# A dense layer with Mish on one core: the head of the program in smaller pieces (x tiles 0 and 1, k 0 of w1)

## The chip, the core and the metric

The kernel runs on one core of one Trainium2 chip. Time is device time in microseconds (us) of one execution; what is compared is the median over runs. The core's engines are TensorE (PE, with its weight loads listed apart as PEld), VectorE (DVE), ScalarE (ACT), GpSimd (POOL) and SyncE (SP). SP and ACT each have a ring (a queue) from which 16 DMA engines take transfers.

## The reference: two matrix products with Mish between

```python
B, S, D, F = 1, 2048, 512, 1792          # all inputs bf16
h = jnp.einsum("bsd,df->bsf", x, w1) + b1
sp = jnp.log1p(jnp.exp(-jnp.abs(h))) + jnp.where(h > 0, h, jnp.zeros_like(h))
act = h * jnp.tanh(sp)
return jnp.einsum("bsf,fd->bsd", act, w2)
```

## The kernel before

The 2048 rows of x are four blocks of 512. Within a block, the first product makes h transposed: w1 is the stationary side, in 4 slices of 128 along D (called k 0 to 3) and 14 slices of 128 along F (called f 0 to 13); xT, x transposed, is the moving side. Each (block, f) adds four products of k 0 to 3 into one bank of PSUM, and ScalarE reads the bank, adds b1 and applies Mish into `a_sb`. The second product takes `a_sb` as the stationary side and w2 as the moving one, 14 products for each tile of 128 rows; VectorE copies the bank out and SP stores it. All blocks go through PE in the order in which the code is written: first products of block 0, second products of block 0, first products of block 1 and so on. There is no planner: each engine takes its instructions in the order of the code, and waits are semaphore counts (`wait`, `mark`).

Only the head, block 0, is special. Its 512 rows are four tiles of 128, called tile 0 to 3 (`j` or `js` in the code).

- Tiles 2 and 3, and all later blocks, come in transposed by a DMA transpose. Tiles 0 and 1 come as they are into `x_nat` and are transposed on PE against an identity matrix (`ident`), in halves of 64 rows (`transpose_x`, product at L147), 16 small products; VectorE and ScalarE copy the results from PSUM to xT (L155).
- While these loads are under way PE runs 7 filler products on constants (L105, sizes in `WARM`).
- For f 0 to 7 (`OPEN` = 8, one bank each) w1 comes in four loads, one for each k: k 0 and k 2 on ScalarE's ring (L109 and L110), k 1 and k 3 on SP's (L112 and L115), k 3 behind the DMA transpose of tiles 2 and 3 (L114). That transpose waits for the third filler.
- SP's ring then has b1, w1 for f 8 to 13, w2 and the transposes of blocks 1 to 3.
- `first(fs, js, ks)` (L239) writes products of block 0 for those f, tiles and k; `mm1_step` (L168) puts the waits ahead of each: the bank, the load of w1, the copy of xT.

Tiles 0 and 1 are read with two neighbouring rows of x in one partition: partition p holds row 2p as tile 0 and row 2p + 1 as tile 1, so one load of 256 KB has rows of 2 KB. `rows` (L191) stores these two tiles accordingly.

Of the kernel before, what the change touches and what calls it, by code (L numbers as in the profile page):

```python
# [4 lines left out]

P = 128
SQ = 32
WARM = (512,) * 5 + (256,) * 2
BLOCKS = (512, 512, 512, 512)


# [21 lines left out]
def bass_standalone__dense_activation_mish__prompt_kernel(  # L33
# [16 lines left out]
    x2, out2 = x[0], out[0]  # L50
# [3 lines left out]
    OPEN = 8  # L54
    N0 = BLOCKS[0] // P

    with ExitStack() as es:
        def sb(name, shape, t):
            return es.enter_context(nc.sbuf_tensor(name, shape, t))

        x_nat = sb("x_nat", [P, 2, D], BF)
        xT = sb("xT", [P, KT, S], BF)
# [6 lines left out]
        ident = sb("ident", [P, P], BF)  # L69
        a_sb = sb("a_sb", [P, FT, S], BF)  # L70
        o_sb = sb("o_sb", [P, S // P, D], BF)
        ps = es.enter_context(nc.psum_tensor("ps", [P, 8, 512], F32))

        def sem(name):
            return es.enter_context(nc.semaphore(name))

        sp = Stream(nc.sync, None)
        pe = Stream(nc.tensor, sem("c_pe"))
        dve = Stream(nc.vector, sem("c_dve"))
        act = Stream(nc.scalar, sem("c_act"))  # L80
        pool = Stream(nc.gpsimd, sem("c_pool"))

        def load(q, dst, src, name, transpose=False):
            s = sem(name)
            (q.eng.dma_start_transpose if transpose else q.eng.dma_start)(dst, src).then_inc(s, 16)
            return (s, 16)

        def load_w1(q, ks, a, b):
            return load(q, w1_sb[:, ks, a * P:b * P], w1v[:, ks, a * P:b * P], "s_w1_%d_%d" % (ks.start, a))
# [6 lines left out]
        def load_part(q, k0, k1, a, b):  # L96
            t = load_w1(q, slice(k0, k1), a, b)
            for f in range(a, b):
                for k in range(k0, k1):
                    t_w1[k, f] = t  # L100
# [3 lines left out]
        c_m = nc.const_aps.tensor(1.0, [P, 512], BF)  # L104
        t_fill = [pe.mark(nc.tensor.matmul(ps[:, 7, 0:n], c_w, c_m[:, 0:n], start=True, stop=True)) for n in WARM]  # L105

        act.eng.preload_act_table(ACT.Mish)  # L107
        act.wait(t_bz)
        for k in (0, 2):  # L109
            load_part(act, k, k + 1, 0, OPEN)  # L110
        t_xn = load(sp, x_nat[:, :, :], x2[0:2 * P, :].rearrange("(p j) d -> p j d", p=P), "s_xn")
        load_part(sp, 1, 2, 0, OPEN)  # L112
        sp.wait(t_fill[2])
        t_x23 = load(sp, xT[:, :, 2 * P:4 * P], x2[2 * P:4 * P, :], "s_x23", True)  # L114
# [4 lines left out]
        t = load(sp, w2_sb[:, :, :], w2v, "s_w2")  # L119
# [3 lines left out]
        for s in range(1, len(BLOCKS)):  # L123
            lo, hi = starts[s], starts[s + 1]
# [5 lines left out]
        t_id = dve.mark(nc.vector.tensor_scalar(ident[:, :], diff[:, :], 0, None, ALU.is_equal))  # L130

        free = [[] for _ in range(8)]
        t_cp = {(j, k): t_x23 for j in (2, 3) for k in range(KT)}
        t_mish = {}

        def transpose_x():

            pe.wait(t_xn, t_id)
            H = P // 2
            for b0, eng, js, ks in ((0, dve, (0,), (0,)), (2, act, (1,), (0,)), (4, dve, (0, 1), (1,)), (6, act, (0, 1), (2, 3))):  # L140
                m = len(js)
                for i, k in enumerate(ks):
                    for n, j in enumerate(js):
                        lo = (i * m + n) * H
                        for h in (0, 1):
                            g = slice(h * H, (h + 1) * H)
                            mm = nc.tensor.matmul(ps[:, b0 + h, lo:lo + H], x_nat[g, j, k * P:(k + 1) * P], ident[g, g],  # L147
                                                  start=True, stop=True)
                eng.wait(pe.mark(mm))
                for i, k in enumerate(ks):  # L150
                    dst = xT[:, k, js[0] * P:(js[-1] + 1) * P].rearrange("p (j h t) -> p j h t", j=m, h=2)
                    src = ps[:, b0:b0 + 2, i * m * H:(i + 1) * m * H].rearrange("p h (j t) -> p j h t", j=m)
                    if m == 1:
                        dst, src = dst[:, 0], src[:, 0]
                    t = eng.mark(nc.vector.tensor_copy(dst, src) if eng is dve else act.eng.activation(dst, src, ACT.Copy))  # L155
                    for j in js:
                        t_cp[j, k] = t
                free[b0] = free[b0 + 1] = [t]

        def mish(s, f, bank, t_mm):  # L160
            n = BLOCKS[s]
            act.wait(t_b1c, t_mm)
            t = act.mark(act.eng.activation(a_sb[:, f, starts[s]:starts[s + 1]], ps[:, bank, 0:n], ACT.Mish,  # L163
                                            bias=b1_sb[:, f:f + 1]))
            t_mish[s, f] = t
            free[bank] = [t]

        def mm1_step(s, f, k, bank, js=None):  # L168

            n = BLOCKS[s]  # L170
            lo, hi = (0, n) if js is None else (js[0] * P, (js[-1] + 1) * P)
            first = k == 0 and lo == 0
            if first:
                pe.wait(*free[bank])
            pe.wait(t_w1[k, f])
            if s:
                pe.wait(t_xT[s])
            else:
                pe.wait(*[t_cp[j, k] for j in (js or range(N0))])
            return nc.tensor.matmul(ps[:, bank, lo:hi], w1_sb[:, k, f * P:(f + 1) * P],  # L180
                                    xT[:, k, starts[s] + lo:starts[s] + hi], start=first, stop=(k == KT - 1 and hi == n))
# [8 lines left out]

        def rows(i):  # L191

            if i < 2:
                return out2[0:2 * P, :].rearrange("(p j) d -> p j d", p=P)[:, i, :]
            return out2[i * P:(i + 1) * P, :]

        def mm2_step(i, f, lo, hi, bank):
# [7 lines left out]
        def put(i, lo, hi, bank, t_mm, q=sp):  # L205
            nonlocal n_out
            dve.wait(t_mm)
            t = dve.mark(nc.vector.tensor_copy(o_sb[:, i, lo:hi], ps[:, bank, 0:hi - lo]))  # L208
            free[bank] = [t]
            q.wait(t)  # L210
            q.eng.dma_start(rows(i)[:, lo:hi], o_sb[:, i, lo:hi]).then_inc(s_out, 16)
            n_out += 1
# [8 lines left out]
        def mm2_last(i):  # L221

            nonlocal n_out
            cuts = (0, D - 3 * P // 2, D - P // 2, D)
            toks = []
            for n, eng in enumerate((dve, dve, act)):
                lo, hi, bank = cuts[n], cuts[n + 1], 4 + (i + n) % 4
                for f in range(FT):
                    mm = mm2_step(i, f, lo, hi, bank)
                eng.wait(pe.mark(mm))  # L230
                dst, src = o_sb[:, i, lo:hi], ps[:, bank, 0:hi - lo]
                t = eng.mark(nc.vector.tensor_copy(dst, src) if eng is dve else act.eng.activation(dst, src, ACT.Copy))  # L232
                toks.append((lo, hi, t))
            for q, (lo, hi, t) in zip((sp, sp, act), toks):
                q.wait(t)
                q.eng.dma_start(rows(i)[:, lo:hi], o_sb[:, i, lo:hi]).then_inc(s_out, 16)
                n_out += 1

        def first(fs, js, ks, last=False):  # L239
            for k in ks:  # L240
                for f in fs:
                    mm = mm1_step(0, f, k, f % 8, js)
                    if last and k == KT - 1:
                        mish(0, f, f % 8, pe.mark(mm))


        def spread_b1():
            dve.wait(t_b1)
            for j in range(P // SQ):
                t = dve.mark(nc.vector.transpose(b1_T[j * SQ:(j + 1) * SQ, :], b1_nat[:, j * SQ:(j + 1) * SQ]))  # L250
            dve.wait(t)
            return dve.mark(nc.vector.tensor_copy(b1_sb[:, :], b1_T[:, 0:FT]))  # L252

        transpose_x()
        t_b1c = spread_b1()
        first(range(4), (0,), (0,))
        first(range(4), (1,), (0,))
        first(range(4, OPEN), (0, 1), (0,))
        first(range(OPEN), (0, 1), (1, 2))
        first(range(OPEN), (2, 3), (0, 1, 2))  # L260
        first(range(OPEN), None, (3,), True)
        for f in range(OPEN, FT):
# [41 lines left out]
```

## Time and profile before

| what | value |
|---|---|
| time, median of 3 runs | 105.19 us (105.11 to 105.49) |
| span of the profiled execution, first to last instruction | 102.9 us (no time of it beyond the span is listed; the median is 2.3 above) |
| granted TensorE clock, mean | 1.000 |
| busy: PE / PEld | 100.2 us (97%) / 48.8 us (47%) |
| busy: ACT / DVE | 39.5 us (38%) / 13.1 us (13%) |
| read from HBM / written | 3.94 MB / 2.10 MB |

A row of a list of instructions has line, engine, operation, out<-in and shape. In a timeline a row starts with the start in the span and the length in us. A DMA row gives the size and the us from the issue to the landing of the transfer. In the profile, w1_sb and w2_sb are both called `w_sb`, and b1_nat `b_nat`. A matmul's listed length includes its passage through the array, so the step from one matmul to the next is shorter than its length.

### The profile page before, as it was taken

The page shows a single profiled execution, that of the slowest core. Times are in us where ns is not written, and L with a number is a line of the kernel's source. Part 1 is how long each engine was busy: PE and PEld are TensorE (multiplying, and loading weights), DVE is VectorE, ACT ScalarE, POOL GpSimd, SP SyncE. Part 2 cuts the span into 40 slices and gives each one's busy share as a digit, 9 for nine tenths or more (in the row PEclk, how much of TensorE's full clock was granted, in tenths as well). Part 3 has the DMA queues.
Part 4 walks back from the last instruction along what each step waited for, and adds up shares of the span by engine and source line. Part 5 has one row for each costly group of instructions (what it writes and reads, how often), then busy time and mean ns, then how long its engine had stood idle before and what let it go on. Part 6 is the DMA issues. An engine that isn't in the chain of part 4 may idle for free.

```text
span 102.9 us, 1196 instructions
## 1 busy us (share of the span) xinstructions
PE 100.2 (97%) x527; PEld 48.8 (47%) x527; DVE 13.1 (13%) x26; ACT 39.5 (38%) x61; POOL 0.4 (0%) x5
## 2 busy tenths in 40 slices
PE   6999999999999999999999999999999999999993
PEld 2697444444444444444444444444444444444472
DVE  1203000220220000022220000022201000020241
ACT  4301999000047777000017777400006777700000
POOL 1000000000000000000000000000000000000000
DMA  2999999991110000011001000001111000001112
GB/s 61 375 283 358 363 243 112 269 237 51 51 51 0 0 6 0 0 51 51 20 31 51 0 0 10 0 3 48 51 51 51 0 0 0 0 6 51 51 51 51
DMA packets 12977, 7.94 MB, mean 77 GB/s; under 512 B 7980, under 2 KB 12332, under 8 KB 12972
## 3 DMA queue, kind: packets, MB, share of 16 engines
q1 hardware_dynamic: 12540, 7.33, 27.4%
q10 hardware_dynamic: 432, 0.54, 1.5%
q8 instruction: 4, 0.07, 0.3%
q14 instruction: 1, 0.01, 0.0%
HBM read 3.94 MB, written 2.10 MB: 59 GB/s over the span
## 4 chain that ended last, share of the span: by engine, by line
PE 97%; DVE 0%; ACT 0%; issue 0%
PE ps L180 47%; PE ps L202 47%; PE ps L105 3%; DVE xT L155 0%; ACT o_sb L232 0%; PE ps L147 0%
## 5 line engine op out<-in xcount | busy, mean ns | idle before, releaser
L163 ACT ACTIVATE a_sb<-ps,b_sb 128x512 bf16<-128x512 f32 x56 | 37.1, 698 | 47.9 <-PE ps L180 47.9
L180 PE MATMUL ps<-xT,w_sb 128*128 128x512 bf16 (+2 forms) x252 | 49.1, 355 | 0.2 <-DVE xT L155 0.2
L202 PE MATMUL ps<-w_sb,a_sb 128*128 128x512 bf16 (+3 forms) x252 | 49.1, 355 | 0.0
L180 PEld LDWEIGHTS ps<-xT,w_sb 128*128 128x128 bf16 x252 | 24.2, 98 | 24.1 <-DVE xT L155 0.3
L202 PEld LDWEIGHTS ps<-w_sb,a_sb 128*128 128x128 bf16 x252 | 23.2, 98 | 25.5
L208 DVE CAST o_sb<-ps 128x512 bf16<-128x512 f32 x15 | 10.4, 692 | 79.8 <-PE ps L202 79.8
L232 ACT ACTIVATE o_sb<-ps 128x64 bf16<-128x64 f32 x1 | 0.2, 224 | 11.5 <-PE ps L202 11.5
L105 PE MATMUL ps<-const-bfloat16-1.0 128*128 128x512 bf16 (+1 forms) x7 | 2.7, 566 | 0.8 <-PEq L289 0.8
L105 PEld LDWEIGHTS ps<-const-bfloat16-1.0 128*128 128x128 bf16 x7 | 0.9, 138 | 2.1 <-issue 2.1
L155 ACT ACTIVATE xT<-ps 128x256 bf16<-128x256 f32 (+1 forms) x3 | 0.9, 347 | 1.7 <-PE ps L147 1.7
L107 ACT ACT_TABLE_LOAD x1 | 1.3, 1283 | 0.7 <-PEq L289 0.7
L250 DVE STREAM_TRANSPOSE b_T<-b_nat 32x32 bf16<-32x32 bf16 x4 | 0.8, 202 | 3.3 <-DMA b_nat<-in_b_dram 3.2
L232 DVE CAST o_sb<-ps 128x320 bf16<-128x320 f32 (+1 forms) x2 | 0.8, 392 | 1.5 <-PE ps L202 1.5
L155 DVE CAST xT<-ps 128x128 bf16<-128x128 f32 (+1 forms) x2 | 0.6, 354 | 2.4 <-PE ps L147 2.4
L147 PEld LDWEIGHTS ps<-ident,x_nat 64*128 64x128 bf16 x16 | 0.4, 118 | 0.4 <-DMA x_nat<-in_x_dram 0.4
L147 PE MATMUL ps<-ident,x_nat 64*128 64x64 bf16 x16 | 0.5, 222 | 0.0
L130 DVE TENSOR_SCALAR ident<-diff 128x128 bf16<-128x128 int32 x1 | 0.2, 227 | 0.2 <-POOL diff L128 0.2
L128 POOL IOTA diff<- 128x128 int32 x1 | 0.2, 234 | 0.4 <-POOLq L289 0.4
L102 DVE MEMSET b_nat<- 32x64 uint32 x1 | 0.1, 112 | 0.8 <-PEq L289 0.8
L252 DVE CAST b_sb<-b_T 128x14 f32<-128x14 bf16 x1 | 0.2, 176 | 0.0
L289 POOL MEMSET const-bfloat16-1.0<- 128x1 bf16 x1 | 0.1, 102 | 0.0
L289 POOL MEMSET const-uint8-127<- 128x1 uint8 x1 | 0.1, 102 | 0.0
(2 smaller groups left out, 0.2 us busy)
## 6 DMA issues: line engine op xcount, KB each, us to landing
out_dram<-o_sb SPq DMA_DIRECT2D x15, 128.0 KB, 1.7
w_sb<-in_w_dram SPq DMA_DIRECT2D x1, 1792.0 KB, 10.7
w_sb<-in_w_dram SPq DMA_DIRECT2D x1, 768.0 KB, 6.1
w_sb<-in_w_dram ACTq DMA_DIRECT2D x2, 256.0 KB, 3.7
w_sb<-in_w_dram SPq DMA_DIRECT2D x2, 256.0 KB, 3.7
x_nat<-in_x_dram SPq DMA_DIRECT2D x1, 256.0 KB, 2.6
out_dram<-o_sb SPq DMA_DIRECT2D x1, 80.0 KB, 1.6
xT<-in_x_dram SPq DMA_TRANSPOSE x4, 5.0
```

Source lines behind the costliest of these rows:

```text
L105: t_fill = [pe.mark(nc.tensor.matmul(ps[:, 7, 0:n], c_w, c_m[:, 0:n], start=True, stop=True)) for n in WARM]
L107: act.eng.preload_act_table(ACT.Mish)
L128: t_diff = pool.mark(pool.eng.iota(diff[:, :], pattern=[[1, P]], base=0, channel_multiplier=-1))
L130: t_id = dve.mark(nc.vector.tensor_scalar(ident[:, :], diff[:, :], 0, None, ALU.is_equal))
L147: mm = nc.tensor.matmul(ps[:, b0 + h, lo:lo + H], x_nat[g, j, k * P:(k + 1) * P], ident[g, g], start=True, stop=True)
L155: t = eng.mark(nc.vector.tensor_copy(dst, src) if eng is dve else act.eng.activation(dst, src, ACT.Copy))
L163: t = act.mark(act.eng.activation(a_sb[:, f, starts[s]:starts[s + 1]], ps[:, bank, 0:n], ACT.Mish, bias=b1_sb[:, f:f + 1]))
L180: return nc.tensor.matmul(ps[:, bank, lo:hi], w1_sb[:, k, f * P:(f + 1) * P], xT[:, k, starts[s] + lo:starts[s] + hi], start=first, stop=( ...
L202: return nc.tensor.matmul(ps[:, bank, 0:hi - lo], a_sb[:, f, i * P:(i + 1) * P], w2_sb[:, f, lo:hi], start=(f == 0), stop=(f == FT - 1))
L208: t = dve.mark(nc.vector.tensor_copy(o_sb[:, i, lo:hi], ps[:, bank, 0:hi - lo]))
L232: t = eng.mark(nc.vector.tensor_copy(dst, src) if eng is dve else act.eng.activation(dst, src, ACT.Copy))
L250: t = dve.mark(nc.vector.transpose(b1_T[j * SQ:(j + 1) * SQ, :], b1_nat[:, j * SQ:(j + 1) * SQ]))
```

## The change

x tiles 0 and 1 are plain tiles of 128 rows now, loaded by two transfers of 128 KB with rows of 1 KB; `rows` is simplified with it. k 0 of w1 comes as two loads, f 0 to 3 and f 4 to 7, both on ScalarE's ring, ahead of k 2. One filler of 256 columns is left out. PE transposes tile 0 when tile 0 is there (k 0, then k 1 to 3), then tile 1; VectorE copies k 0 of each tile, ScalarE k 1 to 3 of each tile in one instruction. The first products are written in another order.

```diff
-WARM = (512,) * 5 + (256,) * 2
+WARM = (512,) * 5 + (256,)
+HALF = 4
...
-        for k in (0, 2):
-            load_part(act, k, k + 1, 0, OPEN)
-        t_xn = load(sp, x_nat[:, :, :], x2[0:2 * P, :].rearrange("(p j) d -> p j d", p=P), "s_xn")
+        load_part(act, 0, 1, 0, HALF)
+        load_part(act, 0, 1, HALF, OPEN)
+        load_part(act, 2, 3, 0, OPEN)
+        t_xn = [load(sp, x_nat[:, i, :], x2[i * P:(i + 1) * P, :], "s_xn%d" % i) for i in range(2)]
         load_part(sp, 1, 2, 0, OPEN)
         sp.wait(t_fill[2])
         t_x23 = load(sp, xT[:, :, 2 * P:4 * P], x2[2 * P:4 * P, :], "s_x23", True)
...
-            pe.wait(t_xn, t_id)
             H = P // 2
-            for b0, eng, js, ks in ((0, dve, (0,), (0,)), (2, act, (1,), (0,)), (4, dve, (0, 1), (1,)), (6, act, (0, 1), (2, 3))):
+            pe.wait(t_id)
+            for i in (0, 1):
+                pe.wait(t_xn[i])
+                for eng, b0, ks in ((dve, 2 * i, (0,)), (act, 4 + 2 * i, (1, 2, 3))):
...
-            if i < 2:
-                return out2[0:2 * P, :].rearrange("(p j) d -> p j d", p=P)[:, i, :]
             return out2[i * P:(i + 1) * P, :]
...
-        first(range(4), (0,), (0,))
-        first(range(4), (1,), (0,))
-        first(range(4, OPEN), (0, 1), (0,))
-        first(range(OPEN), (0, 1), (1, 2))
+        first(range(HALF), (0,), (0,))
+        first(range(HALF), (1,), (0,))
+        first(range(HALF), (0, 1), (1,))
+        first(range(HALF, OPEN), (0, 1), (0, 1))
+        first(range(OPEN), (0, 1), (2,))
         first(range(OPEN), (2, 3), (0, 1, 2))
         first(range(OPEN), None, (3,), True)
```

On PE, from the transposes to the products of k 2, before (s_xn, s_xn0 and s_xn1 are the loads of x; s_w1_1_0 is k 1 of w1, s_w1_0_0 and s_w1_0_4 k 0, s_w1_2_0 k 2; c_dve and c_act are the copies):

```order
L147 MATMUL ps<-ident,x_nat 128x64 [waits c_dve,s_xn]
L147 MATMUL ps<-ident,x_nat 128x64 x15
L180 MATMUL ps<-xT,w1_sb 128x128 [waits s_w1_0_0,c_dve]
L180 MATMUL ps<-xT,w1_sb 128x128
L180 MATMUL ps<-xT,w1_sb 128x128 [waits c_act]
L180 MATMUL ps<-xT,w1_sb 128x128 x5
L180 MATMUL ps<-xT,w1_sb 128x256 [waits c_dve]
L180 MATMUL ps<-xT,w1_sb 128x256
L180 MATMUL ps<-xT,w1_sb 128x256 [waits c_act]
L180 MATMUL ps<-xT,w1_sb 128x256
L180 MATMUL ps<-xT,w1_sb 128x256 [waits s_w1_1_0]
```

and in the changed kernel:

```order
L149 MATMUL ps<-ident,x_nat 128x64 [waits s_xn0,c_dve]
L149 MATMUL ps<-ident,x_nat 128x64 x7
L149 MATMUL ps<-ident,x_nat 128x64 [waits s_xn1]
L149 MATMUL ps<-ident,x_nat 128x64 x7
L181 MATMUL ps<-xT,w1_sb 128x128 [waits s_w1_0_0,c_dve]
L181 MATMUL ps<-xT,w1_sb 128x128
L181 MATMUL ps<-xT,w1_sb 128x128 [waits c_dve]
L181 MATMUL ps<-xT,w1_sb 128x128 x5
L181 MATMUL ps<-xT,w1_sb 128x256 [waits c_act,s_w1_1_0]
L181 MATMUL ps<-xT,w1_sb 128x256 x3
L181 MATMUL ps<-xT,w1_sb 128x256 [waits s_w1_0_4]
```

All 16 transposes still stand ahead of the first product, the second eight behind a wait of their own. The wait for k 1 stood four 256-column products behind the eight of 128 columns; now it stands right behind them.

On ScalarE's ring, before and then in the changed kernel:

```order
L85 DMA w1_sb<-in_w1_dram 128x1024 [waits c_dve]
L85 DMA w1_sb<-in_w1_dram 128x1024
L155 ACTIVATE xT<-ps 128x128 [waits c_pe]
L155 ACTIVATE xT<-ps 128x256 [waits c_pe]
L155 ACTIVATE xT<-ps 128x256
```

```order
L86 DMA w1_sb<-in_w1_dram 128x512 [waits c_dve]
L86 DMA w1_sb<-in_w1_dram 128x512
L86 DMA w1_sb<-in_w1_dram 128x1024
L156 ACTIVATE xT<-ps 128x3x128 [waits c_pe] x2
L164 ACTIVATE a_sb<-ps,b1_sb 128x512 [waits c_pe,c_dve]
```

ScalarE issues three loads instead of two, k 2 as the third, and makes two copies of 384 columns instead of three of 128, 256 and 256.

On SP's ring, in the changed kernel, up to w1 for f 8 to 13:

```order
L86 DMA x_nat<-in_x_dram 128x512 [waits barrier_Pool_Activation_PE_DVE_SP_release]
L86 DMA x_nat<-in_x_dram 128x512
L86 DMA w1_sb<-in_w1_dram 128x1024
L86 DMA_TRANSPOSE xT<-in_x_dram 128x4x256 [waits c_pe]
L86 DMA w1_sb<-in_w1_dram 128x1024
L86 DMA b1_nat<-in_b1_dram 14x128 [waits c_dve]
L86 DMA w1_sb<-in_w1_dram 128x4x768
```

Before, one load of x stood where the first two stand now; k 1 has moved from the second place to the third, and from there on the queue is the same.

More of the change, by code (lines that the diff above doesn't have):

```diff
@@ L136, in transpose_x @@
         def transpose_x():
-            pe.wait(t_xn, t_id)
             H = P // 2
-            for b0, eng, js, ks in ((0, dve, (0,), (0,)), (2, act, (1,), (0,)), (4, dve, (0, 1), (1,)), (6, act, (0, 1), (2, 3))):
[L141 to L144, printed above, removed]
+            pe.wait(t_id)
+            for i in (0, 1):
+                pe.wait(t_xn[i])
+                for eng, b0, ks in ((dve, 2 * i, (0,)), (act, 4 + 2 * i, (1, 2, 3))):
+                    m = len(ks)
+                    for n, k in enumerate(ks):
                         for h in (0, 1):
                             g = slice(h * H, (h + 1) * H)
[L147 to L152, printed above, removed]
+                            mm = nc.tensor.matmul(ps[:, b0 + h, n * H:(n + 1) * H], x_nat[g, i, k * P:(k + 1) * P],
+                                                  ident[g, g], start=True, stop=True)
+                    eng.wait(pe.mark(mm))
+                    dst = xT[:, ks[0]:ks[-1] + 1, i * P:(i + 1) * P].rearrange("p k (h t) -> p k h t", h=2)
+                    src = ps[:, b0:b0 + 2, 0:m * H].rearrange("p h (k t) -> p k h t", k=m)
                     if m == 1:
@@ L155, in transpose_x @@
                     t = eng.mark(nc.vector.tensor_copy(dst, src) if eng is dve else act.eng.activation(dst, src, ACT.Copy))
-                    for j in js:
-                        t_cp[j, k] = t
-                free[b0] = free[b0 + 1] = [t]
+                    for k in ks:
+                        t_cp[i, k] = t
+                    free[b0] = free[b0 + 1] = [t]
         def mish(s, f, bank, t_mm):
```

## The prediction, on record before the changed kernel ran

> **What bounds the kernel now.** I read the chain of waits first: what follows what until the end, as start, length and work.
>
> ```profile
> 0.77 2.72 PE ps L105 x7
> 3.49 0.19 PE ps L147 x3
> ...
> 3.70 0.30 DVE xT L155
> ...
> 4.13 12.32 PE ps L180 x84
> 16.45 12.09 PE ps L202 x56
> ...
> 88.97 12.17 PE ps L202 x84
> ```
>
> From 4.13 on TensorE (PE) never stops until it has done all products; nothing but its own work is on the chain. So a change at the head of the program counts by one thing: by how much the unbroken run of products is moved. A stall of PE behind 4.13 is paid in full, and an earlier start is won only if PE doesn't stop again.
>
> Next the list of waits, for what PE waits on before 4.13, and the timeline of the head (start, length, engine, line, work).
>
> ```profile
> PEld ps L147 <- DMA x_nat<-in_x_dram: 0.4, 1, 0.4
> PE ps L180 <- DVE xT L155: 0.2, 1, 0.2
> ```
>
> ```profile
> 3.07 0.42 PE L105 MATMUL ps<-const-bfloat16-1.0 128*128 128x256 bf16 x1
> 3.42 0.42 PEld L147 LDWEIGHTS ps<-ident,x_nat 64*128 64x128 bf16 x16 [0.41 <-DMA x_nat<-in_x_dram]
> 3.70 0.62 DVE L155 CAST xT<-ps 128x128 bf16<-128x128 f32 x2 [2.38 <-PE ps L147]
> 3.75 0.91 ACT L155 ACTIVATE xT<-ps 128x128 bf16<-128x128 f32 x3 [1.74 <-PE ps L147]
> ...
> 4.57 4.97 PE L180 MATMUL ps<-xT,w_sb 128*128 128x256 bf16 x44
> ...
> 9.38 7.07 PE L180 MATMUL ps<-xT,w_sb 128*128 128x512 bf16 x32
> ```
>
> PE waits for x at 3.42 and for the first copy at 4.13; the eight 128-column products fill 4.13 to 4.57 (55 ns each); then come 44 products of 256 columns, 4.57 to 9.38, so 109 ns each. The first four of them are k 0 of f 4 to 7, so k 1 of w1 is first used at 4.57 + 4 x 0.109 = 5.01.
>
> Last the DMA view, in narrow windows, so that one transfer stands in each (size, then us from issue to landing; in this order x, k 0, k 1, k 2, the DMA transpose, the rest of w1):
>
> ```profile
> x_nat<-in_x_dram SPq DMA_DIRECT2D x1, 256.0 KB, 2.6
> ...
> w_sb<-in_w_dram ACTq DMA_DIRECT2D x1, 256.0 KB, 3.0
> w_sb<-in_w_dram SPq DMA_DIRECT2D x1, 256.0 KB, 3.6
> ...
> w_sb<-in_w_dram ACTq DMA_DIRECT2D x1, 256.0 KB, 4.3
> ...
> xT<-in_x_dram SPq DMA_TRANSPOSE x1, 4.4
> ...
> w_sb<-in_w_dram SPq DMA_DIRECT2D x1, 768.0 KB, 6.1
> ```
>
> with the issues themselves:
>
> ```profile
> 0.74 0.40 SPq L85 DMA_DIRECT2D x_nat<-in_x_dram  x1
> 0.95 0.38 ACTq L85 DMA_DIRECT2D w_sb<-in_w_dram  x1
> 1.19 0.42 SPq L85 DMA_DIRECT2D w_sb<-in_w_dram  x1
> 1.36 0.46 ACTq L85 DMA_DIRECT2D w_sb<-in_w_dram  x1
> ...
> 2.24 1.31 SPq L85 DMA_TRANSPOSE xT<-in_x_dram  x1
> ...
> 4.73 0.41 SPq L85 DMA_DIRECT2D w_sb<-in_w_dram  x1
> ```
>
> x is there at 0.74 + 2.6 = 3.34, k 0 at 3.95, k 1 at 1.19 + 3.6 = 4.79, k 2 at 5.66, the transposed tiles 2, 3 at 6.64. Today k 1 has 5.01 - 4.79 = 0.22 us to spare. The transfers pass one after another, as the two queues (q1 is SP's, q10 ScalarE's) show in the windows 2.40 to 2.80, 2.85 to 3.40, 3.60 to 4.00 and 4.40 to 4.80 (packets, MB, share of the 16 engines; of each window the one queue that fills it):
>
> ```profile
> q1 hardware_dynamic: 74, 0.15, 93.6%
> ...
> q10 hardware_dynamic: 101, 0.21, 101.1%
> ...
> q1 hardware_dynamic: 72, 0.15, 100.0%
> ...
> q10 hardware_dynamic: 75, 0.15, 99.0%
> ...
> ```
>
> x, then k 0, then k 1, then k 2: whole transfers in the order of issue, alternating between the rings, on 16 engines that are full. So when k 1 lands depends on the bytes ahead of it: 256 KB of x and 256 KB of k 0.
>
> **The change part by part.** *Loads.* x becomes two loads of 128 KB, k 0 two of 128 KB. By the steps of today's issues (0.45 on SP, 0.41 on ScalarE) they go out at 0.74 and 1.19 on SP and 0.95 and 1.36 on ScalarE; k 1 follows on SP at about 1.64, k 2 on ScalarE at about 1.77. The order of passage is then x 0, k 0 low half, x 1, k 0 high half, k 1, k 2: the bytes ahead of k 1 are the 512 KB of before, now in rows of 1 KB instead of 2 KB. k 1's issue is 0.45 later, which costs nothing by itself: it lands 3.6 after issue against x's 2.6, so about 1.0 of it is queueing, and that covers the 0.45. SP's DMA transpose waits for the third filler matmul and goes out at 2.24 as before, since SP is done with k 1 by 1.64 + 0.42 = 2.06.
>
> What 1 KB rows cost: w2 comes in such rows, and 2 KB rows pass from 2.40 to 3.40 (columns: stretch, its length, busy time and count of PE, PEld, DVE, ACT, POOL, clock, DMA share, GB/s).
>
> ```profile
> 1.60:2.40 0.80, 0.80 (x3) 0.28 (x2) 0.00 (x0) 0.41 (x1) 0.00 (x0) 1.00 0.74 125
> 2.40:3.40 1.00, 1.00 (x4) 0.30 (x2) 0.00 (x0) 0.00 (x0) 0.00 (x0) 1.00 1.01 381
> 10.80:13.40 2.60, 2.60 (x14) 1.16 (x12) 0.00 (x0) 2.60 (x6) 0.00 (x0) 1.00 1.09 358
> ...
> DMA packets 593, 0.61 MB, mean 380 GB/s; under 512 B 2, under 2 KB 593, under 8 KB 593
> ```
>
> 512 KB take 1.38 us at 381 GB/s, 1.46 at 358 (w2 behind 10.80) and 1.38 at 380 (the last row, w2 from 10.00 to 11.60): 0 to 0.09 more. The ramp, 1.60 to 2.40, moves only 125 GB/s, 0.10 MB. If it is a matter of time, 1 KB rows lose nothing there; if it is one of a number of rows, they move 0.05 MB in it, and 0.05 MB at 381 GB/s is 0.13 us. Bounds for k 1: 4.79 to 5.01; I take the middle, 4.90. A gain is not in these bounds, since no byte ahead of k 1 is gone.
>
> A rule of the Trainium skill (DMA: Bandwidth & Descriptors, Issuing engines are not separate DMA queues) speaks against the two rings: transfers from both interleave on the same 16 engines, and only issue time is saved. The queue rows agree that the engines are shared, but show whole blocks, not an even mixture; by an even mixture k 1 would share the engines with k 2, which is a rival below.
>
> *Fillers, transposes, copies.* The weights of the third and of the fifth filler of 512 columns:
>
> ```profile
> 1.58 0.15 PEld L105 LDWEIGHTS ps<-const-bfloat16-1.0 128*128 128x128 bf16 x1 [0.28 <-issue]
> ...
> 2.43 0.15 PEld L105 LDWEIGHTS ps<-const-bfloat16-1.0 128*128 128x128 bf16 x1 [0.28 <-issue]
> ```
>
> So one of 512 columns takes 0.85 / 2 = 0.43, one of 256 columns 0.21. One of 256 goes: PE is free at 3.07 instead of 3.28; today it then waits on to 3.42, so the filler was covered by the wait for x, and without that wait it would be worth 0.21. x 0 can be there a little before 3.34, and its eight transposes (half of the 0.42) go early. But both tiles' transposes stand ahead of all products on PE, so the first product waits for x 1. With k 0's low half ahead, x 1 is the third of three 128 KB pieces: 384 KB must pass where 256 KB sufficed for 3.34. 128 KB at 380 GB/s are 0.34, so x 1 lands at about 3.7, transposes start 0.08 behind (3.42 - 3.34) at 3.78; 3.34 and 3.42 are the lower ends, if x 1 passes right behind x 0. The form of each copy:
>
> ```profile
> L155 DVE CAST xT<-ps 128x128 bf16<-128x128 f32 x1 | 0.3, 292 | 2.4 <-PE ps L147 2.4
> L155 ACT ACTIVATE xT<-ps 128x128 bf16<-128x128 f32 x1 | 0.3, 278 | 1.7 <-PE ps L147 1.7
> L155 ACT ACTIVATE xT<-ps 128x256 bf16<-128x256 f32 x2 | 0.7, 381 | 0.0
> ```
>
> VectorE copies k 0 of x 1: from first transpose to product today 4.13 - 3.42 = 0.71, so 4.49. Two products of x 0 are done by then; the third waits, because f 2 and f 3 accumulate in the banks that held x 1's k 0. Six products of 55 ns follow: PE stands before k 1 at 4.49 + 0.33 = 4.82. ScalarE's copy of x 1's k 1 to 3 ends as late: it starts today 3.75 - 3.42 = 0.33 behind the first of four transposes and now has eight ahead of it, so 0.33 + 4 x 0.026 = 0.44 (0.42 / 16 for one); 384 columns take about 0.48 (278 and 381 give 103 ns per 128 columns); to PE it is 4.13 - 3.70 - 0.29 = 0.14: 3.78 + 0.44 + 0.48 + 0.14 = 4.84. VectorE's second copy of 256 columns is gone, and nothing queues behind it but the spreading of b1.
>
> *Order of the products.* Here is the step that decides. Before, k 0 of f 4 to 7 (4 x 0.109 = 0.44 us) stood between the 128-column products and k 1. Now k 1 of f 0 to 3 stands right behind them, and k 0 of f 4 to 7 after it. PE needs k 1 at 4.82 and has it at 4.90 + 0.08 = 4.98 (bounds 4.87 to 5.09). Behind that wait stands the whole rest: the 4.57 point of before. So the run of products is moved by 4.98 - 4.57 = 0.41; without k 1's wait by 4.82 - 4.57 = 0.25.
>
> *Everything later.* k 2 is needed 12 products on, at 4.98 + 1.31 = 6.29, and lands by 5.66 + 0.22 = 5.88; tiles 2, 3 at 6.29 + 0.87 = 7.16 against 6.86; the rest of w1 (4.73 + 6.1 = 10.83 today) against the end of eight 512-column products, 9.38 + 8 x 0.216 = 11.11 plus 0.41 (12.09 / 56 for one). Their cover is the later PE itself. The Mish row, the second products and the stores are as before; tiles 0 and 1 are stored as plain rows, amid the run, where nobody waits.
>
> The sum: span 102.9 + 0.41 = 103.3. The median, 105.19, is 2.3 above the span, and I leave that as it is: 105.19 + 0.41 = 105.6.
>
> **The rivals.** *k 1 in time*: if the ramp is no longer and the order of blocks leaves k 1 at 4.79, the copies of x 1 set the time, +0.25: 105.4. For it: the bounds touch it. Against: any of the two row-size costs.
>
> *The split pays*: x 1 passes right behind x 0 and k 1 comes with the copies. PE could go on from 3.07 + 0.71 = 3.78 at best, 0.35 before 4.13: 104.8, no further, since the fillers end there. Against: k 1 would have to land near 4.2 with the same bytes ahead.
>
> *k 2 ahead of k 1, or mixed with it* (slower): the blocks alternate by issue, and k 1's new issue at 1.64 is only 0.13 ahead of k 2's 1.77. If ScalarE's third issue is ready first, 256 KB at 381 GB/s, 0.69, pass before k 1: 105.6 + 0.69 = 106.3; an even mixture comes to at most the same. It decides from the point where SP's two small loads take longer than ScalarE's two by 0.13. Against: SP began 0.21 earlier today.
>
> *The clock of PE comes late* (slower). Filler matmuls of 512 columns stand 0.43 apart, the products behind 16.45 12.09 / 56 = 0.216 apart. So PE ran at half rate until some point between 3.07 and 4.13, 2.3 to 3.4 us behind its start (the clock column shows 1.00 throughout and cannot tell). The new head has a filler less and three gaps up to 4.98. If full rate needs the same time again from x 1's transposes at 3.78, it comes at 6.1 to 7.2, and half the work from 4.98 on is lost: 0.6 to 1.1, so about 106.4. The Trainium skill (TensorE: Matmul & The Clock Gate, Part 1) has such a rule: full clock follows about 3.4 us of sustained work, in a free-running window. The trace agrees with that length within its bounds, but no row shows what gaps of 0.5 us do.
>
> **How the numbers follow.** Forecast 0.60, k 1 in time 0.17, the split pays 0.06, k 2 first 0.08, late clock 0.09. About 0.5%, 0.53 us, is what can be told from no change here. The forecast with its bounds (+0.30 to +0.52, and some tenths of spread between runs: 105.11 to 105.49) lies mostly below 105.72; a quarter of it, 0.15, and the two slow rivals, 0.17, make slower 0.32. Faster would need 104.66, beyond the best case: 0.02. The rest, 0.66, is no change. The likeliest time is 105.6; its own range is 105.4 to 105.8. The range of 8 in 10 leaves out the best case and the far part of the slow ones: 105.1 to 106.2.
>
> **What would show it.** x 0's transposes near 3.1 and x 1's near 3.8; a wait of PE on w1 (k 1) right behind the 128-column products, ending at 4.9 to 5.1; the 44 products of 256 columns starting 0.3 to 0.5 later than 4.57; the span near 103.3. Wrong if x 1's transposes start before 3.6, if PE runs from the first product without a gap, if q10 moves k 2 ahead of k 1, or if the 256-column products are 0.2 apart.

## The result and the profile after

The changed kernel takes 109.37 us (median of 6 runs, 108.28 to 109.67) against 105.15 (104.36 to 105.49); the ratio is 1.040, with a 95% interval of 1.034 to 1.046. That is 4.2 us slower; forecast were 0.41 us, with a range that ended at 106.2. The profiled execution's span is 108.0 us; it took 109.28. Single executions of one kernel can lie 1 to 2 us apart (106.42 and 104.77 of run s2 below), so ratios leave out those over 1.5% above the fastest, and what rests on one execution is weaker than a median.

The chain of waits after, as start, length and work:

```profile
1.66 6.26 DMA w_sb<-in_w_dram
7.92 0.04 issue
7.96 13.55 PE ps L181 x76
21.52 12.09 PE ps L201 x56
...
94.03 12.17 PE ps L201 x84
```

From 21.52 on the program is the one of before, 21.52 - 16.45 = 5.07 us later. All of the loss lies ahead of it, in two pieces. First, k 1 of w1, issued at 1.66, lands at 7.92, and PE stands for it. Second, the 76 products behind that take 13.55, where before the same 76 (44 of 256 columns and 32 of 512) took 16.45 - 4.57 = 11.88: 1.67 more. (The profiled execution of before is one of its shortest, so 5.07 is more than the 4.2 between the medians.) The head in the timeline:

```profile
3.21 0.40 PE L149 MATMUL ps<-ident,x_nat 64*128 64x64 bf16 x8
3.80 0.39 PE L149 MATMUL ps<-ident,x_nat 64*128 64x64 bf16 x8 [0.20 <-DMA x_nat<-in_x_dram]
4.13 1.12 PE L181 MATMUL ps<-xT,w_sb 128*128 128x128 bf16 x8
7.96 4.68 PE L181 MATMUL ps<-xT,w_sb 128*128 128x256 bf16 x26 [2.71 <-DMA w_sb<-in_w_dram]
```

Tile 0 is transposed from 3.21, tile 1 from 3.80, and the first product starts at 4.13, where it started before. The run of 256-column products, at 4.57 before, starts at 7.96: 3.39 later. 3.39 + 1.67 = 5.06, the whole difference.

What the transfers did in the meantime, by stretches, first of the kernel before and then of the changed one (the last two columns are the packets' time as a share of that of the 16 DMA engines, and GB/s):

```profile
3.20:4.20 1.00, 0.83 (x20) 0.52 (x19) 0.50 (x2) 0.45 (x2) 0.00 (x0) 1.00 1.04 391
4.20:5.20 1.00, 1.00 (x14) 0.93 (x14) 0.13 (x1) 0.46 (x2) 0.00 (x0) 1.00 1.07 343
```

```profile
3.20:4.20 1.00, 0.81 (x18) 0.55 (x18) 0.41 (x2) 0.49 (x1) 0.00 (x0) 1.00 0.97 160
4.20:5.20 1.00, 1.00 (x8) 0.62 (x8) 0.17 (x1) 0.49 (x1) 0.00 (x0) 1.00 0.70 217
5.20:6.20 1.00, 0.05 (x1) 0.00 (x0) 0.00 (x0) 0.00 (x0) 0.00 (x0) 1.00 2.08 252
6.20:7.20 1.00, 0.00 (x0) 0.00 (x0) 0.00 (x0) 0.00 (x0) 0.00 (x0) 1.00 0.77 125
```

From 3.20 to 4.20 the share is about that of before (0.97 against 1.04), but the engines move 160 GB/s instead of 391. So it is not that more bytes stood ahead of k 1; the bytes passed at under half the rate. The share adds up the times of the packets, and it goes above 1 (2.08 from 5.20 to 6.20), so it doesn't say that the engines were full of work. The single packets in the traces show where the time went. A packet of 2 KB takes 84 ns at the median, before and after. But of the 1 and 2 KB packets that start from 2.50 to 6.00, none takes over 0.3 us before, and 16 of 564 do after, the longest 2.30 us; from 3.20 to 4.20 ten such packets make up 8.7 of the 15.4 us that all packets took.

Each of these loads reports its landing in 16 parts, and PE can use it from the last on. Before, the parts of k 1 come within 0.4 us, 4.45 to 4.83. After, they come from 4.67 to 7.92, and those of k 0's high half from 3.77 to 6.37. So the first part of k 1 is there only 0.2 later than before; what PE stands for is the last.

And PE's clock, in stretches of the changed kernel (the third column from the right):

```profile
4.13:5.10 0.97, 0.97 (x12) 0.69 (x8) 0.24 (x1) 0.50 (x2) 0.00 (x0) 1.00 0.72 210
5.10:7.90 2.80, 0.15 (x2) 0.00 (x0) 0.00 (x0) 0.00 (x0) 0.00 (x0) 1.00 1.20 166
8.00:8.60 0.60, 0.60 (x6) 0.54 (x7) 0.00 (x0) 0.00 (x0) 0.00 (x0) 1.00 1.35 360
8.70:12.00 3.30, 3.30 (x17) 2.24 (x16) 0.98 (x5) 0.00 (x0) 0.00 (x0) 0.50 1.07 368
12.20:16.00 3.80, 3.80 (x31) 2.73 (x29) 0.00 (x0) 1.07 (x2) 0.00 (x0) 1.00 1.10 348
```

Full rate holds for about 0.7 us behind the stall, then a stretch of 3.3 us at 0.50 follows, with half of its work lost: 1.65, which is the second piece. (The 1.00 ahead of the stall isn't to be trusted: the 128-column products there start 107 ns apart, not 55 as before.)

### The profile page after: what moved, and what is told of

The parts are those of the page before. It is cut to its first block, busy times and chain, and to the rows that moved or that the text cites. A ratio compares the mean times of both kernels' runs of the same rounds, so it can differ in the third digit from the quotient of the medians.

```text
span 108.0 us, 1196 instructions
## 1 busy us (share of the span) xinstructions
PE 102.5 (95%) x526; PEld 49.7 (46%) x526; DVE 13.1 (12%) x26; ACT 39.6 (37%) x60; POOL 0.4 (0%) x5
## 4 chain that ended last, share of the span: by engine, by line
PE 91%; DMA 6%; SPq 1%; issue 0%; ACT 0%
PE ps L181 46%; PE ps L201 45%; DMA w_sb<-in_w_dram 6%; SPq L86 1%; ACT o_sb L231 0%
## 5 line engine op out<-in xcount | busy, mean ns | idle before, releaser
L181 PE MATMUL ps<-xT,w_sb 128*128 128x512 bf16 (+2 forms) x252 | 51.4, 367 | 2.7 <-DMA w_sb<-in_w_dram 2.7
L181 PEld LDWEIGHTS ps<-xT,w_sb 128*128 128x128 bf16 x252 | 25.3, 102 | 28.0 <-DMA w_sb<-in_w_dram 3.0
L156 ACT ACTIVATE xT<-ps 128x384 bf16<-128x384 f32 x2 | 1.0, 491 | 1.7 <-PE ps L149 1.6
L156 DVE CAST xT<-ps 128x128 bf16<-128x128 f32 x2 | 0.6, 292 | 2.5 <-PE ps L149 2.5
```

## The experiments

Several theories stand in the expectations below. A: the split of k 0 upsets the transfers. B: the two loads of x do. C: the DMA transpose gets among rows of k 1 and k 2. K and L: the filler that was left out matters for PE's clock, or doesn't. The others are named where they stand. Where a run is given without an interval, its time is one execution, read against that of the kernel before on the same chip (104.7 to 104.9).

### One part undone

Run e1, of the changed kernel:

```diff
-        load_part(act, 0, 1, 0, HALF)
-        load_part(act, 0, 1, HALF, OPEN)
+        load_part(act, 0, 1, 0, OPEN)
```

> The changed kernel with k 0 of w1 as one load of 256 KB again; the two x loads and everything else stay. In the changed kernel k 1 of w1 landed 6.3 us after its issue (7.92), where 4.9 was forecast, and PE stood from 5.0 to 7.96. Theory A (the split of k 0 on ScalarE's ring, three loads there beside SP's, upsets the order in which the 16 engines get through): k 1 lands by 5.2, span 103.0 to 103.6. Theory B (the two loads of x with 1 KB rows do it): k 1 still lands at 7 or later, span 106.5 to 108.5. Theory C (the DMA transpose of tiles 2, 3 gets among rows of k 1 and k 2 that are not through by 2.24 plus its start): five loads ahead of it instead of four before and six in the changed kernel, so between, k 1 at 5 to 8.

Run e2:

```diff
-        t_xn = [load(sp, x_nat[:, i, :], x2[i * P:(i + 1) * P, :], "s_xn%d" % i) for i in range(2)]
+        t_x = load(sp, x_nat[:, :, :], x2[0:2 * P, :].rearrange("(p j) d -> p j d", p=P), "s_xn")
+        t_xn = [t_x, t_x]
...                            # tiles 0, 1 stored as in the kernel before
```

> The changed kernel with x tiles 0 and 1 as one load of 256 KB again (two rows of x in a partition, stored accordingly); k 0 in two loads and the rest stay. Theory A (the split of k 0): k 1 lands at 7 or later, span 106.5 to 108.5. Theory B (the x loads): k 1 lands by 5.2, span 103.0 to 103.6. Theory C (the DMA transpose among k 1 and k 2): k 1's issue is early again, at 1.19, so k 1 should be through before the transpose begins: by 5.0, while k 2 may still be late.

e1: 108.07 us, ratio 1.031 (1.020 to 1.043); k 1 still landed at 1.66 + 5.17 = 6.83. e2: 105.17 us over 8 runs, ratio 1.004 (0.9995 to 1.009); k 1, out at 1.20, landed 3.4 later:

```profile
w_sb<-in_w_dram SPq DMA_DIRECT2D x1, 256.0 KB, 3.4
...
4.33 13.57 PE ps L182 x84
17.89 12.09 PE ps L204 x56
```

PE doesn't stop in e2. So k 0's split isn't enough for the loss (e2) and isn't needed for a late k 1 (e1): A falls as the cause by itself, and B looked right. But x in one load also sends k 1 out 0.46 earlier, so e2 undoes two things at once; and in e1 ScalarE, with two loads, sends k 2 out at 1.36, ahead of k 1, which the changed kernel doesn't. The span of e2 is still 1.4 over 102.9: the 84 products take 13.57 instead of 12.32, since in this execution they ran at half rate until 7.0.

### What passes beside k 1

e3 and e4, of the changed kernel, each one edit; r10, sent later, makes both:

```diff
-        sp.wait(t_fill[2])                    # e3, r10: the DMA transpose waits for k 1
+        sp.wait(t_w1[1, 0])
...
-        load_part(act, 2, 3, 0, OPEN)         # e4, r10: ScalarE's k 2 waits for k 1
+        act.wait(t_w1[1, 0])
+        load_part(act, 2, 3, 0, OPEN)
```

> The changed kernel with SP's DMA transpose of tiles 2, 3 waiting for the landing of k 1 instead of for the third filler; all loads ahead of it as changed. Theory C (the transpose disturbs k 1): k 1 lands at 4.8 to 5.2, PE goes on there, and then waits for tiles 2, 3, which land some 4.4 behind the new issue, about 9.5, against a need of 7.2: span near 105.2. Theories A and B (the small loads themselves): k 1 still lands near 7.9, tiles 2, 3 near 12.5, span over 109.

> The changed kernel with ScalarE's load of k 2 waiting for the landing of k 1; all else as changed. If it is k 2 beside k 1 (two rings each with 2 KB rows at once) that holds k 1 up, k 1 lands by 5.0 and k 2 about 8.5, where PE waits 2 us for it: span near 105.4. Theory C (the transpose): k 1 lands near 7.5 as in the changed kernel, k 2 later still, near 10 or 11, span over 109.

> The changed kernel with both ScalarE's load of k 2 and SP's DMA transpose waiting for the landing of k 1 (one of them alone left k 1 at 6.0 and 6.2). If k 1 is late because of what passes beside and behind it: k 1 lands at 4.8 to 5.2. If it is late by its own place, the third load on SP's ring beside the second half of k 0: 5.8 to 6.3. Tiles 2, 3 come late in both (9.5 to 10.7), so the span says little: 105 to 107.

The first pieces of k 1's transfer in the three chains (start of the issue, length to the landing), e3, e4, r10:

```profile
1.66 4.53 DMA w_sb<-in_w_dram
```

```profile
1.66 4.33 DMA w_sb<-in_w_dram
```

```profile
1.66 3.67 DMA w_sb<-in_w_dram
```

k 1 took 6.26 in the changed kernel, 4.53 without the transpose beside it, 4.33 without k 2, 3.67 without both. Run t2 below, with the loads of the changed kernel, has 5.38, so equal loads differ by 0.9 between two executions; that both neighbours cost something is likely, how much each costs isn't shown. Without both k 1 still landed at 5.33, not at 4.90, and the rate from 3.20 to 4.20 was low (265 GB/s in r10, 233 in e3, 221 in e4). r10 shows that this isn't a lack of engines:

```profile
4.20:5.20 1.00, 0.85 (x8) 0.56 (x6) 0.00 (x0) 0.00 (x0) 0.00 (x0) 1.00 0.21 79
```

At a share of 0.21 and 79 GB/s only remainders of k 0's high half and of k 1 are under way; the parts of k 1 land from 4.43 to 5.33. The landing at 4.8 to 5.2 that was expected for a cause beside k 1 was met in none of the three. The times (107.86, 112.67, 106.67) say little, since what was held back came late itself, in e4 and r10 also ScalarE's copies of xT behind the wait.

### The row size, the layout, the issue time

All of the changed kernel. e5 has both tiles in one load, in rows of 1 KB; e6 two loads, of even and odd rows of x; e7 is e2 with k 1 held back by a wait:

```diff
+        t_x = load(sp, x_nat[:, :, :], x2[0:2 * P, :].rearrange("(j p) d -> p j d", p=P), "s_xn")      # e5
...
+        xv = x2[0:2 * P, :].rearrange("(p j) d -> p j d", p=P)                                          # e6
+        t_xn = [load(sp, x_nat[:, i, :], xv[:, i, :], "s_xn%d" % i) for i in range(2)]                  # e6
...
+        sp.wait(t_fill[1])                    # e7, ahead of k 1, with the x load of e2
```

> The changed kernel with both x tiles in one load, but still as rows of 1 KB (256 rows of 1 KB instead of 128 of 2 KB); everything else as changed. With x in one load of 2 KB rows k 1 landed at 4.57 and the stall was gone. If the 1 KB rows of x are what upsets the transfers: k 1 lands at 6 or later, span 106 to 108.5. If it is the number of loads on SP's ring ahead of the DMA transpose, or the later issue of k 1: k 1 lands by 5.0, span 103.5 to 104.5.

> The changed kernel with x still in two loads of 128 KB, but load 0 with the even rows of x and load 1 with the odd ones (the layout of the kernel before); everything else as changed. If it is the number of loads, or k 1's later issue: k 1 lands at 6 to 8, span 106 to 108.5, as in the changed kernel. If it is where the rows of one tile lie in memory (128 KB in one piece): k 1 lands by 5.2, span 103.5 to 104.5.

> The changed kernel with x in one load of 2 KB rows, and SP's load of k 1 held back until the second filler is done (about 1.8 against 1.20 without the wait and 1.66 in the changed kernel). If what decides is that k 1 goes out only beside or behind ScalarE's k 2, close ahead of the DMA transpose: k 1 lands at 6 or later, span 105.5 to 108. If it is the split of x itself: k 1 lands by 5.2, span 103.5 to 104.8.

e5: 107.35 us, k 1 out at 1.25 and landed at 1.25 + 4.22 = 5.47, between the two expectations and 0.9 behind e2, whose rows are of 2 KB; so 1 KB rows may cost something even with an early issue, but not the whole. e6: 108.83 us, k 1 at 1.66 + 5.15 = 6.81: the place of the rows in memory is not it. e7: 107.89 us, k 1 at 6.84 although x came in one load:

```profile
1.81 5.03 DMA w_sb<-in_w_dram
6.85 0.05 issue
6.89 13.21 PE ps L183 x76
```

So B falls as well: the split of x isn't needed, a late issue of k 1 will do, at least beside a split k 0.

### The kernel before with one edit

e8 has x in two loads (with the stores that go with it), t1 only the 3.5 KB load of b1 moved ahead of k 1, r12 only the last filler left out (the diffs show the loads and the fillers alone).

```diff
-        t_xn = load(sp, x_nat[:, :, :], x2[0:2 * P, :].rearrange("(p j) d -> p j d", p=P), "s_xn")      # e8
+        t_xn = [load(sp, x_nat[:, i, :], x2[i * P:(i + 1) * P, :], "s_xn%d" % i) for i in range(2)]
...
+        t_b1 = load(sp, b1_nat[0:FT, :], b1.rearrange("(j p) -> j p", p=P), "s_b1")                     # t1
         load_part(sp, 1, 2, 0, OPEN)
...
-WARM = (512,) * 5 + (256,) * 2                                                                          # r12
+WARM = (512,) * 5 + (256,)
```

> The kernel before with one edit: x tiles 0 and 1 in two loads of 128 KB, stored accordingly; fillers, k 0 in one load, transposes, copies and order of products as before. If the split of x is enough for the late k 1: k 1 lands at 6 to 7.5, and since PE reaches it at about 5.3 here, span 104.5 to 107, time 106 to 108.5. If it needs the other parts too: span 102.9 to 103.8, time 104.3 to 105.2.

> The kernel before with SP's load of b1 (3.5 KB) moved from behind k 3 to ahead of k 1: k 1 goes out near 1.66 instead of 1.20, right ahead of the DMA transpose; no byte is added, no load split, all else as before. If the issue time decides: k 1 lands at 5.8 to 7, PE stops at about 5.0 for 0.8 to 2, time 105.7 to 107.5. If the bytes ahead decide, as the prediction had it: k 1 lands by 4.95, PE doesn't wait, time within 0.2 of the kernel before.

> The kernel before with the seventh filler (256 columns) left out, nothing else. Theory L (covered by the wait for x, worth nothing): 104.9, within 0.2 of the kernel before. Theory K (the window of PE's clock): in a part of the executions the products run at half rate for a further 2 to 3.4 us, 1 to 1.7 us lost there: median 105.2 to 106.2.

e8: 106.83 us, ratio 1.019 (1.003 to 1.036), k 1 at 1.66 + 5.32 = 6.98. t1: 105.25 us, ratio 1.0045 (0.9986 to 1.0105). In t1, k 1 went out at 1.70, and these are k 2 and k 1, with the rate behind 3.20 and PE's wait:

```profile
w_sb<-in_w_dram ACTq DMA_DIRECT2D x1, 256.0 KB, 3.5
w_sb<-in_w_dram SPq DMA_DIRECT2D x1, 256.0 KB, 4.0
...
3.20:4.20 1.00, 0.77 (x18) 0.39 (x16) 0.47 (x2) 0.42 (x2) 0.00 (x0) 1.00 1.06 397
...
5.70 3.89 PE L180 MATMUL ps<-xT,w_sb 128*128 128x256 bf16 x34 [0.40 <-DMA w_sb<-in_w_dram]
```

k 2, out at 1.36, landed at 4.9; k 1, out at 1.70, at 5.7: they changed places. A load of 3.5 KB, nothing for 16 engines, moved k 1 back by a whole transfer, since it came behind k 2 in the order of issue. The rate stayed at 397 GB/s. So the late issue by itself moves the products by 0.69 (5.70 against 5.01), and 0.12 of that is there before, since x landed a little later in this execution; the stop of PE is below the 0.8 to 2 that was expected, and no rate is lost. In the time it can't be told from nothing (1.0045, with 1 in the interval).

In e8, too, k 2 goes out (1.36) ahead of k 1. Its loads differ from those of t1 by the split of x, with k 1's issue at 1.66 against 1.70 and SP's b1 aside; k 1 landed at 6.98 against 5.7.

r12: 104.90 us over 10 runs, ratio 0.999 (0.9955 to 1.003). L holds: the filler was covered.

r9 asks the same of e2, with the seventh filler back:

> The changed kernel with x in one load of 2 KB rows (no late k 1: 105.17 us, span 104.3, its products at half rate until 7.0 in the profiled execution) and the seventh filler of 256 columns back. Theory K (PE's full rate comes in windows, and 0.21 us less of filler ahead of the wait for x lets one window go by): the products run at full rate from about 4 in most executions, time 104.0 to 104.8, 0.4 to 1.2 under the kernel without it. Theory L (the filler is covered by the wait for x, as the prediction said): time 105.0 to 105.4, half rate until 6 or 7 as often as without it.

r9: 105.06 us, ratio 1.002 (0.9975 to 1.006), against 105.17 of e2; the expected gain of K didn't come. Executions of r9 spread from 104.51 to 107.02.

### The order on the rings

r11 is the changed kernel with SP's order x 0, k 1, x 1. s1 has all loads on SP, in the order x 0, k 0 low, x 1, k 0 high, k 1, k 2, transpose; s2 has k 0 (one load), k 1, k 2 on ScalarE's ring; t3 k 0 low, k 1, k 0 high, k 2 there, and seven fillers:

```diff
+        for k in range(3):                    # s2, with x 0, x 1 and the transpose on SP
+            load_part(act, k, k + 1, 0, OPEN)
...
+        load_part(act, 0, 1, 0, HALF)         # t3, with the same on SP
+        load_part(act, 1, 2, 0, OPEN)
+        load_part(act, 0, 1, HALF, OPEN)
+        load_part(act, 2, 3, 0, OPEN)
```

> The changed kernel with SP's ring in the order x 0, k 1, x 1 (before x 0, x 1, k 1). If whatever SP issues third, near 1.66, gets through late: k 1 lands by 4.9, x 1 (128 KB) at 5 to 7, and PE's transposes of tile 1 wait for it: span 105.5 to 108. If the trouble lies with k 1's rows beside those of k 0 and k 2 wherever they stand: k 1 lands at 6 or later, x 1 by 4.2.

> The changed kernel with all loads on SP's ring, in the same order: x 0, k 0 low, x 1, k 0 high, k 1, k 2, then the DMA transpose. k 1 is issued near 2.6 instead of 1.66, the transpose near 3.5 instead of 2.24. If rows of two rings mixing on the engines is what makes k 1 late: transfers pass one after another, k 1 lands at 4.7 to 5.2, k 2 by 6.0, tiles 2, 3 near 7.9, PE goes on at about 5 and waits some 0.7 for tiles 2, 3: span 103.5 to 105 (with PE's half rate up to 106). If it is the late issue as such: k 1 lands at 7 or later, span over 106.5.

> The changed kernel with k 0 (one load), k 1, k 2 on ScalarE's ring in this order and x 0, x 1 and the DMA transpose on SP's: x stays split, k 1 is issued near 1.36 and has no plain load of w1 beside it on the other ring. Mixing: x 1 by 3.8, k 1 at 4.7 to 5.1, k 2 (beside the transpose) at 6 to 7; span 103 to 104.5. Late issue (k 2 is now the late one, at 1.8): k 1 the same, k 2 at 6.5 or later with PE waiting for it near 6.3: span 104 to 105.5.

> The changed kernel with k 1 taken off SP's ring: ScalarE issues k 0 low, k 1, k 0 high, k 2 (k 1 near 1.36), SP x 0, x 1 and the DMA transpose; seven fillers. If k 1 only has to go out in time: k 1 by 4.9, x 1 by 3.9, k 0 high by 5.3, no stall over 0.5, span 102.9 to 104, time 104.3 to 105.3. If the split loads make trouble wherever k 1 stands: k 0 high or k 2 late by over 1, time over 106.

r11: 109.29 us; k 1, out at 1.20, took 3.0, and x 1, 128 KB out at 1.66, took 4.3 and held the transposes up to 5.98. So with these splits what goes out third on SP is late, whichever it is. s1: 109.06 us; on one ring, with no plain load on the other, k 1 went out only at 2.60, took 4.2 and PE waited until 6.85:

```profile
3.20:4.20 1.00, 0.43 (x11) 0.27 (x12) 0.29 (x1) 0.48 (x1) 0.00 (x0) 1.00 0.89 239
...
6.85 2.96 PE L182 MATMUL ps<-xT,w_sb 128*128 128x256 bf16 x13 [1.23 <-DMA w_sb<-in_w_dram]
```

So two rings whose rows mix aren't needed for a late k 1 (4.7 to 5.2 was expected if they were the cause); s1 sends k 1 out later still, so it doesn't say what mixing adds. s2: 104.77 and 106.42 us, the kernel before 104.68 beside it; the trace is of the longer one. There k 1 took 3.6 from 1.36, the rate was 373 GB/s and PE didn't wait for k 1. x stays split in s2, but nothing is won: x 1 landed at 1.20 + 2.9 = 4.1. t3: 105.58 us (four executions, 104.96 to 107.04), ratio 1.007 (1.000 to 1.014); the trace is of the longest. There k 1 was out at 1.36 but took 4.1, and the rate from 3.20 to 4.20 was 177 GB/s; whether the other three had it isn't on record. None of these beats the kernel before.

### The order of the products

t2 is the changed kernel with the four calls of `first` from the kernel before:

```diff
...
+        first(range(4, OPEN), (0, 1), (0,))
+        first(range(OPEN), (0, 1), (1, 2))
```

> The changed kernel with the first products in the order of the kernel before (k 0 of f 4 to 7 ahead of k 1); loads, fillers, transposes and copies as changed. k 1 lands near 7.9 as in the changed kernel. What the order costs by the prediction is four products, 0.44: time 108.6 to 109.2 against 109.4. If the order also decides whether PE's clock falls during the stall: 107 to 108.

t2: 108.24 us, ratio 1.034 (1.025 to 1.043), 1.1 under the changed kernel and between the two expectations. k 1 landed at 7.04 in its profiled execution, and k 0's high half itself only near 5.9, so that PE waited twice. What part of the 1.1 is the order and what the landing cannot be parted with two runs.

### What the runs say together

One profiled execution of each run. Long packets are those of 1 or 2 KB that start from 2.50 to 6.00 and take over 0.3 us, out of some 450 to 620.

| run | a load ahead split into 128 KB | issue of k 1 | GB/s, 3.20 to 4.20 | long packets | landing of k 1 |
|---|---|---|---|---|---|
| before | no | 1.19 | 391 | 0 | 4.79 |
| t1 | no | 1.70, behind k 2 | 397 | 0 | 5.7 |
| e2 / r9 | k 0 | 1.20 | 362 / 335 | 4 / 4 | 4.6 / 4.6 |
| s2 | x | 1.36 | 373 | 1 | 4.9 |
| e5 | k 0 (x whole, 1 KB rows) | 1.25 | 328 | 8 | 5.47 |
| r11 | x, k 0 | 1.20 | 333 | 6 | 4.2 (x 1 late) |
| t3 | x, k 0 | 1.36 | 177 | 17 | 5.4 |
| e1 / e8 | x | 1.66, behind k 2 | 314 / 260 | 7 / 12 | 6.83 / 6.98 |
| e7 | k 0 | 1.81 | 249 | 11 | 6.84 |
| s1 | x, k 0 | 2.60, one ring | 239 | 20 | 6.80 |
| e3 / e4 / r10 | x, k 0 | 1.66 | 233 / 221 / 265 | 7 / 5 / 6 | 6.19 / 5.99 / 5.33 |
| e6 / t2 / changed | x, k 0 | 1.66 | 271 / 176 / 160 | 11 / 18 / 16 | 6.81 / 7.04 / 7.92 |

Four cases make a square of k 0 whole or split and k 1 early or late: the kernel before, e2 and r9 (split alone, 105.17 and 105.06 us), t1 (late alone, 105.25) and e7 (both, 107.89 in its one execution). A late issue alone costs a change of places; a split alone costs nothing that a few runs can tell; in every run with both the rate is down to between 160 and 314 GB/s, and k 1 lands at 6.8 to 7.9, or at 5.3 to 6.2 where its neighbours are held back. Two runs don't fit a plain rule: t3, with k 1 out in time and the rate down all the same in its longest execution (there k 0's high half is out third and k 2 fourth on their ring), and e5, with k 1 out in time and in at 5.47. Why single packets take so long then is open: it isn't the transpose alone, k 2 alone, the 1 KB rows alone or the place of x's rows in memory, and it doesn't need two rings with plain loads.

## Why the prediction was wrong, step by step

- **What bounds the kernel.** Right: a stall of PE was paid in full, and all behind 21.52 only moved.
- **Transposes and copies.** Right: tile 0 from 3.21 (forecast near 3.1), tile 1 from 3.80 (3.78). The eight products ended at 5.04, not 4.82, since they ran at half rate, 107 ns each; this was hidden by the wait for k 1.
- **The filler at nothing.** Right (r12).
- **Order of the products.** Right as a mechanism: PE waited for k 1 behind the 128-column products, from 5.04. t2 doesn't measure the 0.44 cleanly, since its k 1 landed 0.9 earlier.
- **Loads: "k 1's issue is 0.45 later, which costs nothing by itself".** This is the step that failed. The reason given, that about 1.0 of its way is queueing and covers it, was wrong in two ways. First, in t1, with nothing split, the same shift put k 1 behind k 2 and 0.9 later (5.7 against 4.79). In the changed kernel, though, k 1 still goes out ahead of k 2 (1.66 against 1.85), so a rule of blocks in the order of issue gives no loss there. Second, the step took the rate, 381 GB/s, as given, and the changed kernel moved 160 at the time that counts. The bounds, 4.79 to 5.01, held only the cost of a row at full rate, and left out that the rate could fall: a bound from above was missing. The landing was 7.92, 3.0 behind the forecast. The loads did land in the forecast order, x 1 at 3.76 (forecast 3.7); what broke down is from k 0's high half (6.37) on.
- **The rival of k 2 mixed with k 1**, priced at 106.3. In r10, e3 and e4 k 1 lands 1.7 to 2.6 us sooner when k 2, the transpose or both are held back, but against t2, which has the loads of the changed kernel, only 0.9 to 1.7; so the price of k 2 isn't shown. The rule that the forecast set beside it, of the Trainium skill (DMA: Bandwidth & Descriptors, Issuing engines are not separate DMA queues), has transfers of all rings interleave on the same 16 engines. With all loads on one ring k 1 was late as well (s1, 6.80), so sharing between rings isn't needed for the loss.
- **The late clock.** The rival was at 0.09 and 0.6 to 1.1 us. In the changed kernel 1.67 went to half rate, and in another way: full rate was there at the end of the stall and was withdrawn again, by the clock's records from 8.67 to 12.08. The Trainium skill (TensorE: Matmul & The Clock Gate, Part 1) has a free-running window of about 3.4 us, and half clock behind an idle one. The 3.41 us of the record agree with that length; but PE had stood for 2.9 us only and then worked for 0.7, and in e1 it had stood for 1.9 and lost the same 1.67 (13.55 for the 76 products). e3 stood for 1.7 without such a stretch. A late clock without a stall came too: e2 lost 1.25 to half rate, and e5, which stands for about 0.5, needed 14.07 for the 76 products, 2.19 more than before. So the rival was a real one, apart from the stall, and too cheap.
- **The base.** Right as a median: 105.19 was set, 105.15 came. The 2.3 between it and the profiled span is not time around the span: later executions of the kernel before show a span of 102.9 with 104.23 us, and one of 103.9 with 105.18, so 1.3 lie around the span, and executions differ by 1 us in it. The profiled one was among the shortest.

The chances failed with the same step: 0.32 for slower, and no case beyond about 106.7, because every case let the transfers pass at the rate of before.

## What to carry to other kernels

In a head that fills 16 DMA engines, the issue time of a load that PE needs early is part of its price, even when it seems to be hidden by a queue: 3.5 KB put in front of it cost 0.9 us of landing here. Smaller first loads bring no product earlier while the products still wait for the last of them: tile 0 was transposed 0.2 us earlier, and the first product started at 4.13 as before. If a load has to be split, don't push the load that PE needs next behind the pieces: with k 1 on the other ring (s2) it was in by 4.9, though nothing was won over the kernel before. And put a price on half rate of PE wherever the head changes: 1.25 to 2.2 us in four runs here.

## What was not expected of the hardware

The 16 engines showed a share of 97% and moved 160 GB/s, where the same bytes in fewer loads moved at 391: a 2 KB packet took its usual 84 ns at the median, and ten packets of over 0.3 us made up more than half of the time. And PE's full rate was withdrawn not in the stall but 0.7 us behind its end, for 3.4 us. In the executions of the changed kernel whose clock column shows 1.000 throughout, spans are no shorter (108.1 to 108.3, against 106.9 to 108.0 with 0.984), and e7's 76 products took 13.21 with a clock column of 1.00: the steps between matmuls tell the rate more safely than the column.
